# Retention scores as half-height products in one run per head pair, in a kernel of retention, Fourier mixing and an MLP

## The chip, the core and the metric

The kernel runs on one core of a Trainium2 chip. The core has five engines with a queue of instructions each: PE (TensorE, matrix products from SBUF into PSUM; its weight loads are shown as PEld), DVE (VectorE), ACT (ScalarE), POOL (GpSimd) and SP (SyncE, which here only issues DMAs). PSUM has eight banks of 2 KB a partition; a matrix product writes one bank. The metric is the device time in microseconds (us) of one execution, as the median over several runs; lower is better.

## What is computed

Four batches, eight heads, 768 steps, head width 64; a model width of 512 and a hidden width of 2048:

```python
gamma = 1.0 - 2.0 ** (-5.0 - np.arange(H))
for t in range(S):                       # retention, a decayed sum of outer products
    state = gamma * state + einsum('bhd,bhe->bhde', k[:, :, t], v[:, :, t])
    y[:, :, t] = einsum('bhd,bhde->bhe', q[:, :, t], state) / sqrt(D)
x = y, heads side by side                # (4, 768, 512)
u = x + real(fft(fft(x, axis=1), axis=2))
un = (u - mean(u)) / sqrt(var(u) + 1e-6)
out = u + maximum(un @ w_ch1, 0) @ w_ch2
```

The kernel does not run the recurrence step by step. It cuts the 768 steps into six chunks of 128. Within a chunk, y is a masked product of scores (q times k, transposed) with v; what earlier chunks give comes through a state per chunk, built from products of k and v.

## The kernel before

**Order of the work.** Batch one's attention and Fourier part are written out by hand (FIRST). After that the MLP of batch b, two row blocks of 384 rows, is the main stream on PE: 16 hidden products (`h_unit`, 4 matmuls of 384 columns each, evicted with the ReLU to `ht16` by ACT or DVE), then 12 parts of the second layer (`ch_unit`, line 1121, 4 matmuls of 512 columns each, evicted at line 1125 and stored by SP). Between these units, `emit` places the units of batch b+1's attention, its Fourier stages and the normalising. Each stream of units gets a start and an end in units of batches (the tables DM, TS, DA, LD, HT at the top), its units are spread evenly between the two, and all units are emitted in order of the position. Emission is the priority: the framework's scheduler may move an instruction of an engine past one that, by its own reckoning, has to wait. Each engine then works in its fixed order.

**Attention of batches two to four** goes by head pairs (index i from 0 to 3). The steps of `attn_steps` hold: `cast_unit` (POOL: q, k with its decay, v to f16), `kv_unit` (5 products, evicted by one ACT copy and four DVE operations at line 683 that also decay the running state), `y_unit` (22 products of 64 columns into two banks, evicted by two ACT operations at line 716), `t_unit` (q and k transposed) and `a_unit` (scores). In step s stand the cast and the transposes of pair s, the state and scores of pair s-1, and the outputs of pair s-2.

**Scores** (`a_unit`): q transposed is stored as `qTz` in two planes, one for each head of the pair. In each plane the rows of the other head (64 of 128) are zero, so one product of full height, 128 rows by 2 x 128 columns, gives both heads' scores of a chunk at once. There are three parts a pair, spread over time like other units. Each has two such products in a bank and one DVE operation (line 657) that multiplies by the mask and writes the f16 scores `atm`. Batch one has another form (`am_unit`, line 515): products of half height, 64 rows by 128 columns, that use the upper or lower half of the rows for the one or the other head, each head in a bank of its own.

**Transposes** (`t_unit`): in batch two (b < NPE = 2) q and k go through PE (6 transposes each, line 610) and come back by ACT (q in two copies of 64 rows, k in one of 128). In batches three and four two DMA transposes from SP (lines 602 and 604) do it.

**PSUM.** The pool `ps_g` has five banks and serves the scores (`wkA`), `wkK`, `wkY` of batches two to four, the transposes `tq` and `pst`, `ps1` and `pq` of the Fourier stages. `ps_pm` has the other three, for the MLP.

**Second Fourier stage and normalising.** `s2_unit(b, kb)` makes row block kb of u (128 rows): four products, two ACT copies, two DVE sums, two POOL adds of x (lines 1027 and 1029). It then calls `norm_unit`: DVE statistics (lines 1040, 1041) and on ACT the f16 row `un` (line 1042). The buffers of `un` (tag `un16`) are two, in pool `up`. `unT_unit` transposes `un`, by PE for the earlier blocks (line 1065) and by a DMA from SP from block 3 of batch two on (line 1061).

**Loads.** `load_unit` issues the loads of q, k, v of a pair from SP. Those of batch two wait for the seventh weight DMA and a product of batch one; those of later batches wait for `a_of[b - 1, 1]`, the last score product of pair 1 of the batch before.

Of the kernel before, what the change touches and what calls it, by code (L numbers as in the profile page):

```python
# [12 lines left out]
ALU = mybir.AluOpType  # L13
f32 = mybir.dt.float32
f16 = mybir.dt.float16
# [3 lines left out]
P = 128  # L19
B, H, S, D = 4, 8, 768, 64  # L20
DM = 512
DFF = 2048
NCH = S // P
# [6 lines left out]
PAIR_ORDER = [0, 1, 3, 2]  # L30
# [15 lines left out]
"""  # L46
ON_ACT = {'q': (0, 1, 0), 'kv': (1, 1, 1), 'g': (0, 1, 1), 'gr': (0, 0, 0)}
FB = 1
DM0, DM1 = (0.121, 0.179, 0.253, 0.368), (0.004, 0.137, 0.232, 0.341)
TS0 = (0.269, 0.376, 0.393, 0.441, 0.517, 0.575, 0.665, 0.696)  # L50
TS1 = (-0.040, -0.020, 0.048, 0.585)
DA0, DA1 = (0.034, 0.100, 0.173, 0.180, 0.306, 0.315), (0.063, 0.067, 0.063, 0.158, 0.168, 0.189)
LD0, LD1 = (0.160, 0.263), (-0.370, 0.140)
HT0 = (0.683, 0.767, 0.685, 0.583)
NPE = 2
ACT_ROWS = ((2, 5, 6, 7, 8, 9, 10, 14), (0, 3, 6, 7, 9, 10, 11, 12, 14, 15), (2, 4, 5, 6, 7, 8, 10, 14))


@with_exitstack
def kernel(  # L60
# [9 lines left out]
    nc = tc.nc  # L70
# [3 lines left out]
    def pool(name, bufs, **kw):  # L74
        return ctx.enter_context(tc.tile_pool(name=name, bufs=bufs, **kw))
# [9 lines left out]
    fp = pool("fp", 1)  # L85
    gp = pool("gp", 1)
    up = pool("up", 2)
    qnp = pool("qnp", 1)
    hp_ = pool("hp", 1)
    obp = pool("obp", 3)  # L90
    stt = pool("stt", 2)
    ps_g = pool("ps_g", 5, space=PSUM)
# [13 lines left out]
    maskp = const.tile([P, NHP, 2, P], f32, tag="maskp")  # L106
# [71 lines left out]
    in_of, a_of = {}, {}  # L178
# [417 lines left out]
    def t_unit(b, i):  # L596
        def run():
            st = at[b, i] = {}
            kT = st["kT"] = tp.tile([P, NCH, P], f16, tag="kT", name="kT")
            if b >= NPE:  # L600
                qT = st["qT"] = qts[i % 2]
                nc.sync.dma_start_transpose(qT.rearrange("p h c t -> p (h c) t"),
                                            q16_of[b, i].rearrange("p h c d -> p (h c d)"))
                nc.sync.dma_start_transpose(kT, kd_of[b, i].rearrange("p c h d -> p (c h d)"))
                return
            qT = st["qT"] = qts[i % 2] if b else qts[i % 2][:, 0]
            for dst, src in ((qT, q16_of[b, i]), (kT, kd_of[b, i])):
                tq = ps_g.tile([P, NCH, P], f16, tag="g", name="tq", padded_shape=[P, 8, P])
                for c in range(NCH):
                    nc.tensor.transpose(tq[:, c, :], src[:, c].rearrange("p a b -> p (a b)"),  # L610
                                        ident16)
                if dst is qT:
                    for h2 in range(2 if b else 1):
                        rows = slice(D * h2, D * h2 + D) if b else slice(0, P)
                        dst = qT[rows, h2] if b else qT
                        (nc.scalar.copy if h2 == 0 or ON_ACT["q"][min(b, 2)] else nc.vector.tensor_copy)(
                            dst.rearrange("p c t -> p (c t)").rearrange(
                                "p (t c) -> p t c", c=NCH),
                            tq[rows].rearrange("p c t -> p t c"))
                else:  # L620
                    nc.scalar.copy(dst, tq)
        return run
# [23 lines left out]
    def a_unit(b, i, part):  # L646
        def run():
            st = at[b, i]
            if part == 0:
                st["atm"] = ap_.tile([P, NCH, 2, P], f16, tag="atm", name="atm")  # L650
            wk = ps_g.tile([P, 2, 2, P], f32, tag="g", name="wkA")
            for c2 in range(2):
                c = 2 * part + c2
                mm = nc.tensor.matmul(wk[:, c2], st["kT"][:, c, :], st["qT"][:, :, c, :],  # L654
                                      start=True, stop=True)
            a_of[b, i] = mm
            nc.vector.tensor_tensor(  # L657
                out=st["atm"][:, 2 * part:2 * part + 2], in0=wk,
                in1=maskp[:, PAIR_ORDER[i]].unsqueeze(1).to_broadcast([P, 2, 2, P]),
                op=ALU.mult)  # L660
        return run

    def kv_unit(b, i):
# [230 lines left out]
    lb = {}  # L894
# [30 lines left out]
    def n0_unit(half, eng):  # L925
        def run():
            if ("un", 0) not in lb[0]:
                lb[0]["un", 0] = up.tile([P, 2, 257], f16, tag="un16", name="un16").rearrange(
                    "p a b -> p (a b)")[:, 0:DM]
            sl = slice(256 * half, 256 * half + 256)  # L930
            dst, src, mu = lb[0]["un", 0][:, sl], lb[0]["pq", 0][:, sl], fd[0]["mu"][:, 0:1]
            if eng == "a":
                nc.scalar.activation(dst, src, AF.Identity, bias=mu, scale=-1.0)
            else:
                nc.vector.tensor_scalar(out=dst, in0=src, scalar1=-1.0, scalar2=mu, op0=ALU.mult,
                                        op1=ALU.add)
        return run
# [8 lines left out]

    def n_unit(kb, eng):
        def run():
            un = lb[0]["un", kb] = up.tile([P, 2, 257], f16, tag="un16", name="un16").rearrange(
                "p a b -> p (a b)")[:, 0:DM]  # L950
            src, mu = lb[0]["u"][:, kb], lb[0]["st"][:, kb, 0:1]
            if eng == "a":
                lb[0]["una"] = nc.scalar.activation(un, src, AF.Identity, bias=mu, scale=-1.0)
            else:
                lb[0]["una"] = nc.vector.tensor_scalar(out=un, in0=src, scalar1=-1.0, scalar2=mu,
                                                       op0=ALU.mult, op1=ALU.add)
        return run
# [22 lines left out]
    def s2_unit(b, kb):  # L980
        def run():
            if kb == 0:
                lb[b] = dict(u=up.tile([P, NCH, DM], f32, tag="u32", name="u32"),
                             unT=up.tile([P, 4, S], f16, tag="unT", name="unT"),
                             st=stt.tile([P, NCH, 4], f32, tag="stats", name="stats"))
# [11 lines left out]
            if b >= FB:  # L997
                for n, (o, w) in enumerate(((0, 129), (256, 128), (129, 127), (384, 128))):
                    nc.tensor.matmul(pq[:, o:o + w], gt[:, n, j0:j0 + P], t2[:, n, 0:w],  # L999
                                     start=True, stop=True)  # L1000
# [6 lines left out]
                    out=u[:, kb, 0:256].rearrange("p (m t) -> p m t", t=2), in0=lo, scalar=g0,  # L1007
                    in1=qn[:, 0:256].rearrange("p (m t) -> p m t", t=2), op0=ALU.add, op1=op_lo)
                nc.vector.scalar_tensor_tensor(
                    out=u[:, kb, 256:512].rearrange("p (m t) -> p m t", t=2), in0=updn, scalar=g0,  # L1010
                    in1=qn[:, 256:0:-1].rearrange("p (m t) -> p m t", t=2), op0=ALU.add,
                    op1=op_up)
            else:
                for cb in range(2):
                    nc.tensor.matmul(psP, gt[:, cb, j0:j0 + P], cd16[:, cb, 0:257],
                                     start=(cb == 0), stop=(cb == 1))
                for cb in range(2):
                    nc.tensor.matmul(psQ, gt[:, 2 + cb, j0:j0 + P], sd16[:, cb, 1:256],
                                     start=(cb == 0), stop=(cb == 1))
# [8 lines left out]
                                    in1=x[:, kb, 0, 1:257], op=ALU.add)  # L1028
            nc.gpsimd.tensor_tensor(out=u[:, kb, 256:512], in0=u[:, kb, 256:512],  # L1029
                                    in1=x[:, kb, 1, 257:1:-1], op=ALU.add)  # L1030
            norm_unit(b, kb)()
        return run

    def norm_unit(b, kb):
        def run():
            u, stats = lb[b]["u"], lb[b]["st"]
            bst = stt.tile([P, 6], f32, tag=f"bst{kb % 3}", name="bst")
            un = up.tile([P, 2, 257], f16, tag="un16", name="un16").rearrange(
                "p a b -> p (a b)")[:, 0:DM]
            nc.vector.bn_stats(bst, u[:, kb, :])  # L1040
            nc.vector.bn_aggr(stats[:, kb, 0:2], bst)  # L1041
            nc.scalar.activation(un, u[:, kb, :], AF.Identity, bias=stats[:, kb, 0:1], scale=-1.0)  # L1042
            lb[b]["un", kb] = un
        return run
# [12 lines left out]
    def unT_unit(b, kb):  # L1057
        def run():
            un, unT = lb[b].pop(("un", kb)), lb[b]["unT"]
            if b > 1 or b and kb >= 3:  # L1060
                nc.sync.dma_start_transpose(unT[:, :, kb * P:(kb + 1) * P], un)
                return
            pst = ps_g.tile([P, 4, P], f16, tag="g", name="pst", padded_shape=[P, 8, P])
            for cb in range(4):
                nc.tensor.transpose(pst[:, cb, :], un[:, cb * P:(cb + 1) * P], ident16)
            if (kb % 2 == 0) != (b == 0 and kb < 3):
                nc.vector.tensor_copy(unT[:, :, kb * P:(kb + 1) * P], pst)
            else:
                nc.scalar.copy(unT[:, :, kb * P:(kb + 1) * P], pst)
        return run  # L1070
# [162 lines left out]
                    gr=gr_unit, xe=x_edges)[kind](*n)  # L1233

    def mix_units(b, kbs):
        return [s2_unit(b, kb) for kb in kbs], [unT_unit(b, kb) for kb in kbs]

    def emit(streams):
        ev = []
# [19 lines left out]
    for b in range(B):  # L1259
# [17 lines left out]
        if b + 1 < B:  # L1277
            steps = attn_steps(b + 1)
            if b == 0:
# [3 lines left out]
                streams.append(([pad_unit], HT0[2], HT0[3]))  # L1283
                ts = TS0
            else:
                streams.append(([load_unit(b + 1, i) for i in range(4)], b + LD1[0], b + LD1[1]))
                n = [len(u) for u in steps[1:]]
                ts = list(TS1[:2]) + [TS1[2] + TS1[3] * sum(n[:j]) / sum(n) for j in range(6)]
            streams.append((steps[0], b + ts[0], b + ts[1]))
# [38 lines left out]
```

## Time and profile before

| what | value |
|---|---|
| median of 3 runs | 245.68 us (245.26 to 245.90) |
| the profiled execution: its own time | 246.28 us |
| its span, first to last instruction | 244.1 us |
| granted TensorE clock | 1.00 in every stretch |
| score products, line 654 | 72 of 128x256, 57.1 to 174.1 us |
| score evictions, line 657 | 36 of 128x512, 0.680 us each |
| second layer, line 1121 | 89.1 us busy |
| hidden products, line 1078 | 81.9 us busy |
| batch two's attention fed by loads, 52 to 62 us | 258 GB/s, PE busy 8.67 of 10 us |

Times within the execution count from the span's first instruction. A matmul's row overlaps the next one's (its end is modelled, and it is pipelined), so what PE spends on one is read from start to start. In a row of groups, "x6" means six instructions in a row. A row of waits has the engine that waited, the line, who released it, and us in total, how many times, and the longest.

### The profile page before, as it was taken

What the parts mean: (1) busy time and instruction counts of PE and PEld (TensorE: products, weight loads), DVE (VectorE), ACT (ScalarE), POOL (GpSimd) and SP (SyncE); (2) the same over time, 40 slices, a digit from 0 to 9 for tenths busy, and PEclk for the clock granted to TensorE, in tenths of its full rate; (3) what the DMA queues carried; (4) which work ended last, traced back from release to release, by engine and by line L of the source; (5) the groups of instructions that cost most, each with busy time, mean ns of one, the idle gap of its engine ahead of it and who ended that gap; (6) DMA issues with size and microseconds to landing.
All of it is one profiled execution on the core that took longest, in us unless ns stands there. A gap on an engine that the chain in (4) does not pass through costs nothing.

```text
span 244.1 us, 5274 instructions
## 1 busy us (share of the span) xinstructions
PE 231.0 (95%) x2010; PEld 144.6 (59%) x2010; DVE 173.6 (71%) x423; ACT 121.3 (50%) x268; POOL 83.5 (34%) x151
## 2 busy tenths in 40 slices
PE   4499999997999998999999999999999999999995
PEld 1376779755775645665567446665666455445543
DVE  8879987947887788995985748887895556424112
ACT  5989758755785434842247515732257317202500
POOL 7578802456500067690000736660002305000000
PEclk9999999999999999999999999999999999999999
DMA  7997999999999388999999478585100441221012
GB/s 176 232 271 104 199 201 203 221 245 260 268 237 216 69 172 190 182 187 139 262 269 217 92 161 196 118 143 134 72 0 0 46 150 23 43 89 43 1 43 89
DMA packets 99209, 36.39 MB, mean 149 GB/s; under 512 B 89840, under 2 KB 96240, under 8 KB 99184
## 3 DMA queue, kind: packets, MB, share of 16 engines
q1 hardware_dynamic: 94960, 31.86, 63.2%
q0 software_dynamic: 4224, 4.19, 10.8%
q8 instruction: 16, 0.26, 0.5%
q14 instruction: 9, 0.07, 0.1%
HBM read 27.26 MB, written 6.29 MB: 137 GB/s over the span
## 4 chain that ended last, share of the span: by engine, by line
PE 79%; DVE 7%; ACT 4%; DMA 3%; POOL 3%; issue 1%; SPq 1%; POOLq 0%; ACTq 0%; DVEq 0%
PE psc L1121 34%; PE psh L1078 27%; PE wkA L654 3%; DMA v<-in_v_dram 3%; PE ps L837 3%; PE wkY L708 2%; PE pq L999 2%; PE wkY L704 1%; PE wkK L673 1%; PE tq L610 1%; PE ps L817 1%; SPq L209 1%; DVE bst L1040 1%; PE pq L911 1%; DVE atm L529 1%
## 5 line engine op out<-in xcount | busy, mean ns | idle before, releaser
L1121 PE MATMUL psc<-w,ht 128*128 128x512 f16 (+2 forms) x400 | 89.1, 370 | 0.1
L1078 PE MATMUL psh<-unT,w 128*128 128x384 f16 x448 | 81.9, 326 | 0.4 <-ACT ht L1082 0.2
L1121 PEld LDWEIGHTS <-ht 128*128 128x128 f16 x400 | 37.5, 98 | 36.8 <-issue 0.2
L1078 PEld LDWEIGHTS <-w 128*128 128x128 f16 x448 | 42.3, 98 | 24.6 <-issue 1.6
L1082 ACT ACTIVATE ht<-psh 128x384 f16<-128x384 f32 x64 | 30.9, 490 | 40.3 <-PE psh L1078 39.7
L1027 POOL TENSOR_TENSOR u<-u,x 128x256 f32<-128x256 f32 x21 | 13.3, 635 | 106.0 <-DVE u L1006 90.1
L1125 DVE SCALAR_TENSOR_TENSOR ob<-psc,stats,u 128x512 f32<-128x512 f32 (+2 forms) x25 | 18.1, 725 | 25.9 <-PE psc L1121 25.7
L1084 DVE TENSOR_SCALAR ht<-psh 128x384 f16<-128x384 f32 x48 | 26.1, 548 | 8.6 <-PE psh L1078 8.2
L657 DVE TENSOR_TENSOR atm<-wkA,maskp 128x512 f16<-128x512 f32 x36 | 23.9, 683 | 2.5 <-PE wkA L654 2.4
L1042 ACT ACTIVATE un<-u,stats 128x512 f16<-128x512 f32 x21 | 15.1, 721 | 17.9 <-DVE stats L1041 11.5
L683 DVE SCALAR_TENSOR_TENSOR s<-s,gk,wkK 128x128 f16<-128x128 f16 x48 | 16.2, 339 | 6.1 <-ACT s L679 5.5
L1040 DVE BATCH_NORM_STATS2 bst<-u 128x6 f32<-128x512 f32 x21 | 14.6, 694 | 8.3 <-POOL u L1029 8.1
L716 ACT ACTIVATE x<-wkY,gexp 128x384 f16<-128x384 f32 x24 | 12.8, 580 | 9.9 <-PE wkY L708 9.9
L431 POOL TENSOR_SCALAR kd<-k,gexp 128x384 f16<-128x384 f32 x24 | 13.8, 585 | 3.7 <-DMA k<-in_k_dram 2.8
L1029 POOL TENSOR_TENSOR u<-u,x 128x256 f32<-128x256 f32 x21 | 13.3, 635 | 2.4 <-DVE stats L1041 2.4
L654 PE MATMUL wkA<-qTz,kT 128*128 128x256 f16 x72 | 13.3, 273 | 0.1
L1095 PEld LDWEIGHTS <-w 128*128 128x128 f16 x192 | 11.0, 98 | 0.8 <-issue 0.3
L1095 PE MATMUL psh<-unT,w 128*128 128x128 f16 x192 | 11.4, 219 | 0.1
L1001 ACT COPY qn<-pq 128x128 f32<-128x128 f32 x18 | 4.9, 274 | 12.6 <-PE pq L999 11.9
L1006 DVE SCALAR_TENSOR_TENSOR u<-pq,g,qn 128x256 f32<-128x256 f32 x18 | 8.5, 472 | 3.1 <-PE psh L1078 2.5
L436 POOL TENSOR_SCALAR v<-v 128x768 f16<-128x768 f32 x12 | 10.0, 831 | 1.5 <-DMA v<-in_v_dram 1.5
L654 PEld LDWEIGHTS <-kT 128*128 128x128 f16 x72 | 6.9, 98 | 5.6 <-PE psh L1078 0.4
(177 smaller groups left out, 317.4 us busy)
## 6 DMA issues: line engine op xcount, KB each, us to landing
q<-in_q_dram SPq DMA_DIRECT2D x16, 384.0 KB, 6.0
k<-in_k_dram SPq DMA_DIRECT2D x16, 384.0 KB, 6.0
v<-in_v_dram SPq DMA_DIRECT2D x16, 384.0 KB, 6.1
out_dram<-ob SPq DMA_DIRECT2D x23, 256.0 KB, 2.4
w<-in_moe_w_ch_dram POOLq DMA_DIRECT2D x8, 512.0 KB, 11.6
unT<-un SPq DMA_TRANSPOSE x15, 2.4
out_dram<-ob SPq DMA_DIRECT2D x1, 192.0 KB, 1.9
qTz<-q16z SPq DMA_TRANSPOSE x8, 3.8
```

The source lines that it names most:

```text
L431: kc = nc.gpsimd.tensor_scalar(out=kd[:, :, h2, :], in0=k32[:, h2], scalar1=gkd[:, h0 + h2:h0 + h2 + 1], scalar2=1.0, op0=ALU.mult, op1=AL ...
L654: mm = nc.tensor.matmul(wk[:, c2], st["kT"][:, c, :], st["qT"][:, :, c, :], start=True, stop=True)
L657: nc.vector.tensor_tensor(out=st["atm"][:, 2 * part:2 * part + 2], in0=wk, in1=maskp[:, PAIR_ORDER[i]].unsqueeze(1).to_broadcast([P, 2, 2, ...
L683: nc.vector.scalar_tensor_tensor(out=s16[:, c], in0=s16[:, c - 1], scalar=gk2[:, hp:hp + 1], in1=wk[:, c - c0], op0=ALU.mult, op1=ALU.add)
L1040: nc.vector.bn_stats(bst, u[:, kb, :])
L1042: nc.scalar.activation(un, u[:, kb, :], AF.Identity, bias=stats[:, kb, 0:1], scale=-1.0)
L1078: nc.tensor.matmul(psh, w116[:, cb, fb * P:(fb + 1) * P], unT[:, cb, rt * 384:(rt + 1) * 384], start=(cb == 0), stop=(cb == 3))
L1082: nc.scalar.activation(ht16[:, fb, :], psh, AF.Relu, bias=0.0, scale=-1.0)
L1084: nc.vector.tensor_scalar(out=ht16[:, fb, :], in0=psh, scalar1=-1.0, scalar2=0.0, op0=ALU.mult, op1=ALU.max)
L1095: mm = nc.tensor.matmul(psh[:, f], w116[:, cb, fb * P:(fb + 1) * P], unT[:, cb, kb * P:(kb + 1) * P], start=(cb == 0), stop=(cb == 3))
L1121: nc.tensor.matmul(psc[:, c0:c1], ht16[:, fb, rb3 * P:(rb3 + 1) * P], w216[:, fb, c0:c1], start=(fb == 0), stop=(fb == NFB - 1))
L1125: nc.vector.scalar_tensor_tensor(out=ob[:, c0:c1], in0=psc[:, c0:c1], scalar=lb[b]["st"][:, rb, 3:4], in1=lb[b]["u"][:, rb, c0:c1], op0=AL ...
```

## The change

- `a_unit`: part 0 now issues all 12 products of the pair in one run, in the half-height form, into four banks of `ps_g` (three chunks of one head each), and evicts two of them; part 1 evicts the third, part 2 the fourth. Each eviction is 128x384. `a_of`, on which later loads wait, is now the last product of part 0.
- `KD = (3,)`: in batch two, k of pair index 3 is transposed by a DMA from SP; q of that pair stays on PE.
- A pool `unp` of three buffers for `un16`, out of `up`, which had two.
- `s2_unit` no longer calls `norm_unit`. `mix_units` makes turns: turn j issues the sums of the j-th row block, then the normalising of the one before; the last turn issues that of its own block too.
- New numbers in all tables of positions. In order of emission, among others: batch two's pair 1 is transposed one second-layer unit later; batch two's units from kv of pair 2 to the scores of pair 2 stand together without an MLP unit between them; the three DMA transposes of the second half's rows come in reverse order (their stream's end lies before its start); batch one's three last sums stand together.

```diff
-DM0, DM1 = (0.121, 0.179, 0.253, 0.368), (0.004, 0.137, 0.232, 0.341)
-TS0 = (0.269, 0.376, 0.393, 0.441, 0.517, 0.575, 0.665, 0.696)
-TS1 = (-0.040, -0.020, 0.048, 0.585)
-DA0, DA1 = (0.034, 0.100, 0.173, 0.180, 0.306, 0.315), (0.063, 0.067, 0.063, 0.158, 0.168, 0.189)
-LD0, LD1 = (0.160, 0.263), (-0.370, 0.140)
-HT0 = (0.683, 0.767, 0.685, 0.583)
+DM0, DM1 = (0.127, 0.128, 0.261, 0.279), (0.010, 0.137, 0.260, 0.244)
+TS0 = (0.244, 0.368, 0.422, 0.439, 0.519, 0.521, 0.682, 0.695)
+TS1 = (-0.057, 0.016, 0.048, 0.582)
+DA0, DA1 = (0.077, 0.142, 0.177, 0.182, 0.296, 0.312), (0.057, 0.080, 0.086, 0.169, 0.147, 0.204)
+LD0, LD1 = (0.154, 0.258), (-0.365, 0.158)
+HT0 = (0.635, 0.743, 0.599, 0.590)
 NPE = 2
+KD = (3,)
...
+    unp = pool("unp", 3)
...
             for dst, src in ((qT, q16_of[b, i]), (kT, kd_of[b, i])):
+                if dst is kT and i in KD:
+                    nc.sync.dma_start_transpose(kT, src.rearrange("p c h d -> p (c h d)"))
+                    continue
...
             if part == 0:
                 st["atm"] = ap_.tile([P, NCH, 2, P], f16, tag="atm", name="atm")
-            wk = ps_g.tile([P, 2, 2, P], f32, tag="g", name="wkA")
-            for c2 in range(2):
-                c = 2 * part + c2
-                mm = nc.tensor.matmul(wk[:, c2], st["kT"][:, c, :], st["qT"][:, :, c, :],
-                                      start=True, stop=True)
-            a_of[b, i] = mm
-            nc.vector.tensor_tensor(
-                out=st["atm"][:, 2 * part:2 * part + 2], in0=wk,
-                in1=maskp[:, PAIR_ORDER[i]].unsqueeze(1).to_broadcast([P, 2, 2, P]),
-                op=ALU.mult)
+                wk = st["wk"] = [ps_g.tile([P, 3, P], f32, tag="g", name="wkA",
+                                           padded_shape=[P, 4, P]) for _ in range(4)]
+                for c in range(NCH):
+                    for h2 in range(2):
+                        sl = slice(D * h2, D * h2 + D)
+                        mm = nc.tensor.matmul(wk[2 * (c // 3) + h2][:, c % 3],
+                                              st["kT"][sl, c, :], st["qT"][sl, h2, c, :],
+                                              start=True, stop=True)
+                a_of[b, i] = mm
+            for n in ((0, 1), (2,), (3,))[part]:
+                half, h2 = n // 2, n % 2
+                nc.vector.tensor_tensor(
+                    out=st["atm"][:, 3 * half:3 * half + 3, h2], in0=st["wk"][n],
+                    in1=maskp[:, PAIR_ORDER[i], h2].unsqueeze(1).to_broadcast([P, 3, P]),
+                    op=ALU.mult)
...
-            norm_unit(b, kb)()
...
     def mix_units(b, kbs):
-        return [s2_unit(b, kb) for kb in kbs], [unT_unit(b, kb) for kb in kbs]
+        def turn(j):
+            def run():
+                if j < len(kbs):
+                    s2_unit(b, kbs[j])()
+                for n in kbs[max(j - 1, 0):j] + (kbs[-1:] if j == len(kbs) - 1 else []):
+                    norm_unit(b, n)()
+            return run
+        return [turn(j) for j in range(len(kbs))], [unT_unit(b, kb) for kb in kbs]
```

More of the change, by code (lines that the diff above doesn't have):

```diff
@@ L927, in run @@
             if ("un", 0) not in lb[0]:
-                lb[0]["un", 0] = up.tile([P, 2, 257], f16, tag="un16", name="un16").rearrange(
+                lb[0]["un", 0] = unp.tile([P, 2, 257], f16, tag="un16", name="un16").rearrange(
                     "p a b -> p (a b)")[:, 0:DM]
@@ L948, in run @@
         def run():
-            un = lb[0]["un", kb] = up.tile([P, 2, 257], f16, tag="un16", name="un16").rearrange(
+            un = lb[0]["un", kb] = unp.tile([P, 2, 257], f16, tag="un16", name="un16").rearrange(
                 "p a b -> p (a b)")[:, 0:DM]
@@ L1037, in run @@
             bst = stt.tile([P, 6], f32, tag=f"bst{kb % 3}", name="bst")
-            un = up.tile([P, 2, 257], f16, tag="un16", name="un16").rearrange(
+            un = unp.tile([P, 2, 257], f16, tag="un16", name="un16").rearrange(
                 "p a b -> p (a b)")[:, 0:DM]
```

## The prediction

> **What bounds the kernel now.** I read the page's header, its busy shares and the chain of waits first.
>
> ```profile
> span 244.1 us, 5274 instructions
> PE 231.0 (95%) x2010; PEld 144.6 (59%) x2010; DVE 173.6 (71%) x423; ACT 121.3 (50%) x268; POOL 83.5 (34%) x151
> PE 79%; DVE 7%; ACT 4%; DMA 3%; POOL 3%; issue 1%; SPq 1%; POOLq 0%; ACTq 0%; DVEq 0%
> ```
>
> PE holds 79% of the chain that ended last, and the page's forty slices show it at nine tenths or more from the third to the last but one, two excepted. So from about 36 us on, an edit is worth what it takes from PE's issue time, plus what it does to the few waits in which PE stands still. The waits that PE itself or its weight loads had after 46 us come next (waited for, us, times, longest), and with them one DVE row:
>
> ```profile
> PE tq L610 <- POOL kd L431: 1.3, 1, 1.3
> PE pst L1065 <- ACT un L1042: 0.7, 1, 0.7
> PE psh L1078 <- ACT ht L1082: 0.2, 1, 0.2
> PE psh L1078 <- DVE ht L1084: 0.2, 1, 0.2
> PEld L708 <- DVE atm L657: 0.7, 3, 0.3
> DVE bst L1040 <- POOL u L1029: 7.8, 16, 0.9
> ```
>
> Two of them are single holes, one in batch two's attention, one before batch two's second row block. The last row is not PE's, but DVE stands 7.8 us in its queue for POOL, with PSUM evictions behind it. Counted from start to start of PE's matmuls, and with a product charged its columns at the rate of its own undisturbed row (512 columns 0.216 us), I get 6.5 us of PE standing still between 36 us and the end, an estimate. So more than about 6 us cannot come from waits.
>
> **Price of the score products.** The timeline of PE has the old form in batch two (first), and in batch one the half-height form that the change brings (second); columns are start, length, engine, line, operation, tiles, shape.
>
> ```profile
> 57.14 0.38 PE L654 MATMUL wkA<-qTz,kT 128*128 128x256 f16 x2
> 57.36 1.03 PE L1121 MATMUL psc<-w,ht 128*128 128x512 f16 x4
> 58.23 0.60 PE L654 MATMUL wkA<-qTz,kT 128*128 128x256 f16 x4
> 58.66 1.03 PE L1121 MATMUL psc<-w,ht 128*128 128x512 f16 x4
> ```
>
> ```profile
> 19.24 0.59 PE L817 MATMUL ps<-ssp,xab 128*128 128x193 f16 x5
> 19.77 0.51 PE L515 MATMUL wkA<-qTz,kT 64*128 64x128 f16 x12
> 20.21 0.26 PE L817 MATMUL ps<-csp,xab 128*128 128x193 f16 x1
> ```
>
> Old: four products take 58.66 - 58.23 = 0.43 us, so six per head pair 0.65 us. New: the five products of 193 columns ahead of the run start 0.086 us apart (18 of line 837 take 1.54 us in the chain), so they are through at 19.24 + 0.43 = 19.67, and the next full-height product starts at 20.21. The whole run of twelve cost 0.54 us. Six pairs at 0.056 us (128 columns: six transposes start 56.80, the next row 57.14) are 0.34 us, so two half-height products must have run side by side, and about 0.10 us went into each of the change from full to half height and the change back. **Saving: 0.65 - 0.54 = 0.11 us a pair, 12 pairs, 1.4 us.** A broken run is dearer: in batch one a run of six stood 0.24 us between its first two pairs (starts 24.45 and 24.75), and one of twelve some 0.50 us after its seventh (seven products from 15.07 on, the other five from 15.93). With every run broken by 0.24 us the item would turn to +1.5 us. I take three of twelve broken, +0.7 us.
>
> The Trainium skill, "TensorEngine Tiling (Array Packing)", Key Properties, says that a change of the tiling mode drains the array; the two tenths around the run agree with it, and they are why twelve in one run is priced and not three runs of four. By its up to 2x alone, without the drain, the item would be 12 x (0.65 - 0.33) = 3.8 us; the row decides.
>
> **Eviction of the scores.** Before, three operations of 128x512 at line 657, 0.680 us each (2.04 us a pair). After, four of 128x384; the nearest row is line 529, the same width from PSUM with a float mask, 0.547 us (2.19 us). DVE gets 12 x 0.15 = 1.8 us more. What hides it: in 52 to 62 us DVE is busy 5.14 of 10 us, but 8.71 in 62 to 72, 8.29 in 102 to 112 and 9.20 in 150 to 160. Price on PE between 0 and 1.8 us; I take +0.2, since DVE's time comes back partly with the turns below.
>
> **k of pair index 3 of batch two by DMA.** Six transposes of 128 columns leave PE: 6 x 0.057 = 0.34 us, and one ACT copy of 0.80 us. PE no longer waits for that kd cast either (it ended at 66.19 on POOL, and PE reached it at 67.0). SP gets one more transpose: issue 1.2 to 1.95 us, landing 2.7 to 4.6 us by the eight rows of line 604. It stands in SP's queue between batch three's loads and three output stores and waits there for the kd cast. Behind it are the loads of batch three, first needed at about 91 us, and stores that nobody waits for; the buffers of ob are three. Its first reader, the scores of pair 3, starts at 72.2 us, 6 us after the cast. Cover enough: 0 on the path. If it were gone, PE would stand for what is missing of 1.5 + 4.6 us, so up to 1 us. **-0.3 us.**
>
> **Third row buffer.** The hole at 93 us, in the timeline:
>
> ```profile
> 92.30 0.61 PE L1065 MATMUL pst<-ident,un 128*128 128x128 f16 x8
> 92.81 0.72 ACT L1042 ACTIVATE un<-u,stats 128x512 f16<-128x512 f32 x1 [0.47 <-PE pst L1065]
> 93.58 0.40 PE L1065 MATMUL pst<-ident,un 128*128 128x128 f16 x4 [0.68 <-ACT un L1042]
> ```
>
> The third normalised row waits until the first two are transposed, because there are two buffers of un16; its statistics were done at 92.0. With a third buffer it runs at once and ends near 92.75, and two units of new due times lie in between. **-0.7 us** of 0.84. The 1.7 us that ACT waited once for a transpose by DMA goes too, but off the path.
>
> **New turns of the normalising.** The statistics of row block n are now issued after the sums of block n+1, so DVE no longer stands behind POOL's two adds (0.635 us each). What PE lost to this order, by starts: 0.37 us at 203.8 and 0.33 at 208.1 (the two rows with ht above), 0.24, 0.23 and 0.21 between 152 and 156.5: 1.38 us. Bounds 0 and -1.4; I take half, **-0.7**, because the framework already moves such operations past each other. In the third block of each half two rows are normalised in a row, and the first of them is later than before by one turn; the readers (transposes, then 16 hidden products) are four or more products away. The three transposes unT by DMA now go out in reverse, so on SP the last row block's un holds back the two others: about 0.65 x 7 = 4.6 us after its sums, against a chain of 0.95 DVE + 1.3 POOL + 0.9 DVE + 0.72 ACT = 3.9 us. Cover thin, price up to 0.5 us a batch if it fails, taken 0.
>
> **New due times.** Working out the order of emission from both sets of numbers, the first large difference is at the hole of 55 us:
>
> ```profile
> 54.97 0.50 PE L610 MATMUL tq<-ident,q16z 128*128 128x128 f16 x6
> 56.80 0.51 PE L610 MATMUL tq<-ident,kd 128*128 128x128 f16 x6 [1.33 <-POOL kd L431]
> ```
>
> PE stands 1.49 us for the cast of k of pair 1, and that for its load (issued 49.47, median landing 6.0 us, cast started 55.59). The loads are gated by the same weight DMA as before and come no earlier; but pair 1's transposes are emitted one unit of four 512-column products later, which fills 4 x 0.216 = **-0.86 us** of the hole. Against it: batch two's step with kv(2), y(1), t(3) and the scores of pair 2 is now emitted with no large product in between. It needs 2 + 2 + 1 + 4 = 9 banks out of a pool of five. The y banks are freed by two ACT operations of 0.58 us, the kv banks by four DVE operations of 0.34 us. Between nothing (y and transposes, 0.64 + 0.34 us, cover it) and 1.5 us; I take **+0.5**. Batch one's three transposes for row blocks 3 to 5 move ahead of its second product; they cost the same 12 x 0.057 us and their un can be early, since POOL's adds now follow one another: 0. The tables and pads that move by a few units stay in DVE's free time of 72 to 82 us (8.72 of 10 busy): 0.
>
> **Sum.** -1.4 + 0.7 + 0.2 - 0.3 - 0.7 - 0.7 - 0.86 + 0.5 = -2.6 us. The profiled execution took 246.28 us, 244.1 of it span and 2.2 around it, which nothing here changes: 243.7 us. It is 0.6 us over the median of the three runs, 245.68, so against that: **243.1 us**.
>
> **Rivals.** (a) *Banks.* The run takes four of five banks at once, and the last two are evicted one and two units after the first. PE works in order, so a run that waits for a bank holds every product behind it. For it: the two broken runs above, both in batch one. Against it: y is emitted two units ahead of the scores, at about 1 us a unit. All gains without it are 1.4 + 0.3 + 0.7 + 0.7 + 0.86 - 0.2 = 3.8 us; it decides from 3.8 / 12 = 0.31 us a run. At the 0.50 us of the worse row: 245.68 - 3.8 + 6.0 = 247.9 us, slower. The skill's same page, PSUM Bottleneck, warns that faster products leave the eviction as the limit; it would be seen here as this case. (b) *All holes close*: the score saving whole, -1.4 - 0.3 - 0.84 - 1.38 - 1.49 = -5.4, 240.3 us. (c) *The gain moves on*: batch two is fed by loads (258 GB/s in 52 to 62 us), and PE, arriving sooner, waits for the next pair's casts or for DVE: only 0.3 us is left, 245.4 us. Against it: batches three and four show no wait for a load. (d) *The halves do not run side by side*: each run 12 x 0.056 + 0.2 = 0.87 us, so the main sum plus 12 x 0.33 = 4.0: 247.1 us. Against it: the same order and banks as in batch one, where they do.
>
> **How the numbers follow.** Mine 0.50, (a) 0.18, (b) 0.15, (c) 0.13, (d) 0.04. About 0.3% (0.74 us) is what a measurement of this kernel can tell from no change. Faster: mine but for 0.02 that end near the old time, (b), and 0.04 of (c): 0.67. Within: 0.02 and 0.09 of (c): 0.11. Slower: (a) and (d), 0.22. Mine alone spans 241.5 to 244.7. The range goes from the floor of (b), 240.3, to just under (a), 247.2, which leaves out some 0.15.
>
> **What would show it.** Right: score products as pairs of starts some 4 ns apart and runs near 0.54 us; no wait of pst for un; the hole at tq shrunk to about 0.6 us; fewer than 7.8 us of bst waiting for POOL; PE's standing still after 36 us down from 6.5 to about 4 to 5. Wrong: score products with starts broken inside a run, PE waiting for x, s or atm at a score product, or a new PE wait on unT.

## The result, and the profile after

The changed kernel is slower: 246.75 us (median of 5 runs, 246.31 to 247.85) against 245.50 before, a ratio of 1.0052 with a 95% interval of 1.0036 to 1.0068. The profiled execution is the slowest of the five, 247.85 us with a span of 245.7. From its page, the shares by engine and the head of the chain:

```profile
PE 232.8 (95%) x2076; PEld 142.4 (58%) x2076; DVE 175.5 (71%) x435; ACT 120.9 (49%) x267; POOL 83.4 (34%) x151
PE 83%; DMA 5%; DVE 4%; ACT 3%; POOL 1%; SPq 1%; issue 1%; DVEq 0%; ACTq 0%
```

PE was 79% of the chain and is 83%. Three of the forecast's waits are gone, as the waits after 36 us show (first PE's own, then the DVE row):

```profile
PE wkA L661 <- DMA qTz<-q16z: 1.7, 1, 1.7
PE psh L1087 <- ACT ht L1091: 0.3, 1, 0.3
PE pst L1074 <- ACT un L1051: 0.3, 1, 0.3
...
DVE bst L1049 <- POOL u L1039: 2.8, 8, 0.5
```

The hole before k's transposes (1.3 us) is not in the list, pst waits 0.3 us for un and no longer at 93 us, and DVE's statistics (`bst`) wait 2.8 us for POOL where they waited 7.8. In their place stands a wait that no term of the forecast had: a score product, the first of pair 3 of batch three, waits 1.7 us for q transposed by DMA.

```profile
118.28 1.46 PE L1130 MATMUL psc<-w,ht 128*128 128x512 f16 x6
121.44 0.51 PE L661 MATMUL wkA<-qTz,kT 64*128 64x128 f16 x12 [1.70 <-DMA qTz<-q16z]
```

To see where the rest went, I counted PE from start to start of its matmuls, from batch one's first hidden product to the last product of the kernel. A product counts its columns at the rate of its own undisturbed row; "score products" is all time from a score product to the next start and what PE lost right ahead of one, so the changes of height and the waits are in it; "other standing" is what PE lost elsewhere. Times are in us, from the profiled executions.

| kernel | runs come in | score products | other standing | other products |
|---|---|---|---|---|
| before | 33 pieces, full height | 8.25 | 6.24 | 193.37 |
| after | 20 pieces | 11.29 | 4.12 | 193.03 |
| e1 scores only | 19 | 11.53 | 5.24 | 193.37 |
| e2 scores undone | 34, full height | 9.85 | 4.59 | 193.03 |
| e3 later gate | 20 | 9.53 | 4.13 | 193.03 |
| e5 fenced | 12 | 11.59 | 5.19 | 193.03 |
| e8 half where whole | 5 whole, 19 full | 8.64 | 4.01 | 193.03 |
| e9 and loads later | 5 whole, 19 full | 7.67 | 3.96 | 193.03 |

After against before: -2.12 us of standing, -0.34 of other products, and **+3.04 us on the score products**. Ahead of the run that waits for q stand 1.86 us. About 0.10 of this is the change of height that stands ahead of every half-height run (the same holds for such figures below), so 1.77 us is the wait. The two profiled executions differ by two things more: batch one, whose instructions up to there are the same, reached its first hidden product at 33.77 us and not 33.19 (it lies between 33.1 and 34.3 in the profiled executions of all kernels here), and the end is 0.43 us longer (below).

Why the scores cost more stands in PE's timeline of batch two, pair 0 (first) and pair 3 (second):

```profile
57.78 0.34 PE L661 MATMUL wkA<-qTz,kT 64*128 64x128 f16 x6
58.05 0.39 PE L1130 MATMUL psc<-w,ht 128*128 128x512 f16 x1
58.37 0.34 PE L661 MATMUL wkA<-qTz,kT 64*128 64x128 f16 x3
58.64 0.60 PE L1130 MATMUL psc<-w,ht 128*128 128x512 f16 x2
59.18 0.34 PE L661 MATMUL wkA<-qTz,kT 64*128 64x128 f16 x3
59.45 0.39 PE L1130 MATMUL psc<-w,ht 128*128 128x512 f16 x1
```

```profile
72.67 0.51 PE L661 MATMUL wkA<-qTz,kT 64*128 64x128 f16 x12
73.11 0.50 PE L1087 MATMUL psh<-unT,w 128*128 128x384 f16 x2
```

Pair 3's run is whole: 0.44 us, and 0.10 before it. Pair 0's is in three pieces with second-layer products between. Each piece takes 0.27 us, whether it has six products (three pairs side by side) or three (one bank, one half of the rows, no partner), and about 0.10 us ahead: 512 columns starting at 58.05 are through at 58.27, the piece starts at 58.37. That is 3 x 0.37 = 1.1 us, against 0.65 in the old form.

### The profile page after: what moved, and what is told of

Same layout as the page of the kernel before. It is cut to its first block, busy times and chain, and to the rows that moved or that the text cites. A ratio compares the mean times of both kernels' runs of the same rounds, so it can differ in the third digit from the quotient of the medians.

```text
span 245.7 us, 5404 instructions
## 1 busy us (share of the span) xinstructions
PE 232.8 (95%) x2076; PEld 142.4 (58%) x2076; DVE 175.5 (71%) x435; ACT 120.9 (49%) x267; POOL 83.4 (34%) x151
## 4 chain that ended last, share of the span: by engine, by line
PE 83%; DMA 5%; DVE 4%; ACT 3%; POOL 1%; SPq 1%; issue 1%; DVEq 0%; ACTq 0%
PE psc L1130 33%; PE psh L1087 30%; PE wkA L661 3%; DMA v<-in_v_dram 3%; PE ps L847 3%; DMA qTz<-q16z 2%; PE ps L827 2%; PE pq L1009 2%; PE wkY L718 2%; PE wkK L683 1%; PE wkY L714 1%; PE tq L491 1%; PE pq L921 1%; SPq L211 1%; PE tq L615 1%
## 5 line engine op out<-in xcount | busy, mean ns | idle before, releaser
L1087 PEld LDWEIGHTS <-w 128*128 128x128 f16 x448 | 41.4, 98 | 25.9 <-issue 1.2
L667 DVE TENSOR_TENSOR atm<-wkA,maskp 128x384 f16<-128x384 f32 x48 | 24.1, 546 | 1.6 <-PE wkA L661 1.6
L1051 ACT ACTIVATE un<-u,stats 128x512 f16<-128x512 f32 x21 | 14.6, 719 | 11.2 <-DVE stats L1050 7.5
L1104 PEld LDWEIGHTS <-w 128*128 128x128 f16 x192 | 11.1, 98 | 1.2 <-issue 0.7
L661 PE MATMUL wkA<-qTz,kT 64*128 64x128 f16 x144 | 8.7, 218 | 1.8 <-DMA qTz<-q16z 1.7
L661 PEld LDWEIGHTS <-kT 64*128 64x128 f16 x144 | 5.1, 94 | 8.3 <-issue 7.6
L689 ACT CAST s<-wkK 128x128 f16<-128x128 f32 x12 | 3.2, 267 | 11.8 <-issue 8.4
```

Of the source, the lines that this page charges most:

```text
L661: mm = nc.tensor.matmul(wk[2 * (c // 3) + h2][:, c % 3], st["kT"][sl, c, :], st["qT"][sl, h2, c, :], start=True, stop=True)
L667: nc.vector.tensor_tensor(out=st["atm"][:, 3 * half:3 * half + 3, h2], in0=st["wk"][n], in1=maskp[:, PAIR_ORDER[i], h2].unsqueeze(1).to_br ...
L1087: nc.tensor.matmul(psh, w116[:, cb, fb * P:(fb + 1) * P], unT[:, cb, rt * 384:(rt + 1) * 384], start=(cb == 0), stop=(cb == 3))
L1104: mm = nc.tensor.matmul(psh[:, f], w116[:, cb, fb * P:(fb + 1) * P], unT[:, cb, kb * P:(kb + 1) * P], start=(cb == 0), stop=(cb == 3))
```

## The experiments

Each was timed beside the kernel before on the same chip; ratios are to that. Theories: S, broken runs; T, late transposes by DMA; U, batch one's transposes moved ahead of their rows; rivals B (banks) and L (loads).

**e1, the new scores alone in the kernel before.** The edit is the change's `a_unit` and nothing else.

> The kernel before with the new score products alone (runs of twelve half-height products into four banks; old tables, two row buffers, old turns, k by PE). In its order on PE the twelve runs come out in 19 pieces. Theory S (broken runs: a piece costs 0.19 us of change of height, and a piece of three products runs one after the other): products cost 9.2 us against 7.9 of the old form, so 245.5 + 1.3 = 246.8 us. Theory T (the slowdown is the late q transpose of pair 3 of batch three, because the loads of batch four are let go earlier): the gate has moved here too, so up to +1.9 more, or 247.4 alone. The forecast's term (-1.4 saved, +0.7 for broken runs, +0.2 eviction): 245.0 us.

Measured: 248.89 us, 1.0138 (1.0124 to 1.0152). The score part alone loses 3.3 us, two more than its pieces; the rest is PE standing in or ahead of runs. T is not it: no wait for a transpose of q is in the profile. The longest stop, by the timelines of PE and ACT:

```profile
107.05 0.39 PE L656 MATMUL wkA<-qTz,kT 64*128 64x128 f16 x7
108.93 0.32 PE L656 MATMUL wkA<-qTz,kT 64*128 64x128 f16 x5 [1.49 <-ACT x L721]
```

```profile
107.68 0.72 ACT L1047 ACTIVATE un<-u,stats 128x512 f16<-128x512 f32 x1 [1.41 <-DMA unT<-un]
108.31 0.57 ACT L721 ACTIVATE x<-wkY,gexp 128x384 f16<-128x384 f32 x1
```

The run wants the bank of an output y; y's eviction stands on ACT behind a normalised row, and that row waits 1.41 us for one of two row buffers, which a transpose by DMA still reads. The four-bank run thus ties PE to SP's queue. The changed kernel, with its third row buffer, has no such wait in its profile; that the buffer alone cuts the tie was not tested.

**e2, the old scores in the changed kernel.**

> The changed kernel with the old score products (three parts of two full-height products; everything else of the change kept). Theory S: 246.75 - 1.6 = 245.1 us. Theory T: the load gate is the old one again, so the 1.86 us of the wait for q transposed go as well: 243.3 us with both, 244.9 with T alone. The forecast's term: the score part was a gain, so 247.2 us.

Measured: 245.94 us, 1.0014 (1.0004 to 1.0024). Most of the loss goes with the scores. But T's part of the expectation was wrong: with the old gate PE still waits 0.95 us for q transposed at 118 us. Of the 1.44 us between the two rows of the table, 0.8 is that shorter wait and 0.6 the products: in this order of work full-height scores stand for other things too (8.90 us without the wait, against 8.25 before).

**e3, a later gate for the loads.**

```diff
-                a_of[b, i] = mm
-                nc.vector.tensor_tensor(
+                a_of[b, i] = nc.vector.tensor_tensor(
```

> The changed kernel, with the loads of the next batch gated by the last score eviction of pair 1 in place of the last product of its run; SP's order then has the q transpose of pair 3 of batch three ahead of one load more, as before the change. Theory T: the wait of PE for q transposed, 1.86 us in the profile, shrinks below 0.7 us, 245.3 to 246.0 us. Theory S: nothing of its cost is touched, 246.75 us within 0.4.

Measured: 246.19 us, 1.0019 (1.0005 to 1.0032), and in the profile nothing is left of the 1.86 us. SP's issues, after (first) and here:

```profile
112.83 1.23 SPq L606 DMA_TRANSPOSE kT<-kd  x1
114.10 0.57 SPq L191 DMA_DIRECT2D q<-in_q_dram  x1
114.73 0.72 SPq L191 DMA_DIRECT2D k<-in_k_dram  x1
115.54 3.77 SPq L604 DMA_TRANSPOSE qTz<-q16z  x1
```

```profile
112.60 1.23 SPq L606 DMA_TRANSPOSE kT<-kd  x1
113.92 0.53 SPq L191 DMA_DIRECT2D q<-in_q_dram  x1
114.55 2.76 SPq L604 DMA_TRANSPOSE qTz<-q16z  x1
```

With two loads ahead the transpose landed 5.8 us after its issue, at 121.3, when PE had been ready since 119.6. With one ahead it was issued 1.0 us earlier and landed after 5.2; without loads ahead (pair 3 of batch four) it takes 3.7. T is shown. It is worth 0.6 us by the medians and 0.8 by the ratios, less than the wait in the profiled execution, which was the slowest of its five.

**e4, three row buffers and turns alone.**

> The kernel before with three row buffers and the new turns of the normalising alone. Forecast's terms: -0.7 (third buffer, the hole at 93 us) and -0.7 (turns), so 244.1 us. Rival: the framework's order had hidden the turns already and the third row is late for another reason, 245.3 us or more.

Measured: 245.41 us, 0.9994 (0.9986 to 1.0003): no difference. The hole at 93 us is gone, and the one at 55 us is 0.74 us (in this execution PE reached it 0.5 us later and was let go 0.3 us earlier). But products of y wait for score evictions, 0.81 us at 155 and 0.36 at 103; the kernel before stood 0.23 and 0.21 us near 156 and not at 103. It looks as if the turns moved DVE's time from one reader to another; buffer and turns were not timed apart.

**e5, whole runs by force.** Each PE instruction emitted after a run is ordered behind its last product:

```diff
+            for x in tc.nc.cur_bb.bb.instructions[n0:]:
+                if run_end and str(x.engine) == run_end[0]:
+                    tc.add_manual_dep(x, run_end[1],
+                                      mybir.DependencyInfo(mybir.DependencyClass.NoSync,
+                                                           mybir.DependencyReason.DATA),
+                                      reason="behind the run")
```

> The changed kernel, in which every PE instruction emitted after a run of twelve stays behind its last product. In its order on PE all twelve runs are whole (20 pieces before). Theory S (broken runs): the products cost 12 x 0.54 = 6.4 us in place of 9.4, PE does not wait for banks, 243.8 us, or 244.9 with the wait for q transposed still there in full. Rival B (banks: the run was broken because a bank was not free, so a whole run waits as long as its pieces cost): PE waits 0.3 us or more inside most of the eight runs that were broken, 246.4 us or more.

Measured: 248.61 us, 1.0127 (1.0107 to 1.0147). Rival B holds. (Six runs were broken in the changed kernel, not eight as written there.) The runs are whole in order, but PE stands inside four of these six: 0.39 and 0.30 us in pair 0 of batch two, 0.64 in pair 1, 0.31 in pair 2, and in pair 0 of batch four

```profile
151.35 0.34 PE L661 MATMUL wkA<-qTz,kT 64*128 64x128 f16 x6
151.99 0.34 PE L661 MATMUL wkA<-qTz,kT 64*128 64x128 f16 x3 [0.30 <-ACT ht L1092]
153.12 0.32 PE L661 MATMUL wkA<-qTz,kT 64*128 64x128 f16 x3 [0.80 <-DVE u L1020]
```

(The first of the two waits names ACT's `ht`, which frees a bank of the MLP's pool. A DVE operation on the state ended at the same 151.94 us and frees one of `ps_g`, so it may be that one.) So the pieces were not a whim of the order: four of five banks are not free when most of these pairs are due. Standing costs more than breaking: without the wait for q the score products take 10.8 us here and 9.5 in pieces. The Trainium skill, "TensorEngine Tiling (Array Packing)", PSUM Bottleneck, warns that tiling speeds up the products and not the eviction; these waits for evictions agree.

**e6, batch one's old due times.** `DM0 = (0.121, 0.179, 0.253, 0.368)` in the changed kernel, where batch one's transposes and the product behind them wait for their rows, as the profile after has it:

```profile
45.98 0.39 PE L1074 MATMUL pst<-ident,un 128*128 128x128 f16 x4
46.64 0.34 PE L1074 MATMUL pst<-ident,un 128*128 128x128 f16 x3 [0.27 <-ACT un L1051]
47.12 1.05 PE L1104 MATMUL psh<-unT,w 128*128 128x128 f16 x16
```

> The changed kernel with the old due times of batch one's last three row blocks alone (DM0). Theory U (batch one: the transposes moved ahead wait for their rows, 0.43 + 0.31 + 0.13 us at 45 to 47 us): 245.9 us. Rival L (loads: batch two's hole at 55 us was a wait for loads that come no earlier, so what PE loses before it is not lost at the end): 246.75 us within 0.4, and the hole at batch two's first k transposes is there again.

Measured: 246.64 us, 1.0038 (1.0021 to 1.0054). Other standing falls from 4.12 to 3.25 us as U says, but the time hardly moves (0.1 us by the medians, 0.3 by the ratios, and the intervals overlap). L was wrong about the place: the hole at 55 us did not come back. PE, earlier, waits for two transposes by DMA, 0.68 us at 111 (a new wait, for k) and 1.05 at 119 (for q); e10 tests whether the gain is lost there.

**e7, half height only where the run is whole.** Five pairs as in the change, the other seven in the old form (`if (b, i) not in ((1, 3), (2, 2), (2, 3), (3, 2), (3, 3))`, batches counted from 0).

> The changed kernel with half-height products only for five of the twelve pairs (pair 3 of batch two, pairs 2 and 3 of batches three and four), which come out whole in the order on PE; the other seven in the old form. Theory S: 245.94 of the kernel with the old scores less 5 x 0.12 us = 245.4 us. Rival B: these runs too are paid in waits, 245.9 us or more.

Measured: 245.67 us, 0.9994 (0.9981 to 1.0008), between the two; PE waits 1.11 us for q transposed again.

**e8, e7 with batch one's old due times.**

> The kernel of e7 with the old due times of batch one's last three row blocks. Theories S and U together: 245.4 - 0.87 = 244.5 us, below both kernels. Rivals B and L: 245.4 to 245.9 us.

Measured: 244.64 us, 0.9950 (0.9933 to 0.9968). S and U together, as expected. The wait for q is still there, 1.17 us.

**e9, e8 with batch four's loads behind that transpose.** The edit moves these loads and nothing else:

```diff
-                    tc.add_manual_dep(dma.ins, a_of[b - 1, 1].ins.name,
+                    tc.add_manual_dep(dma.ins, a_of[b - 1, 2 if b == 3 else 1].ins.name,
```

> The kernel of e8, with the loads of batch four gated by the scores of pair 2 of batch three in place of pair 1, so that SP issues the q transpose of pair 3 ahead of the first of these loads. Theory T: it lands within about 4 us of its issue in place of 5.3, the wait of 1.17 us before the scores of pair 3 falls below 0.3, 243.6 us. Rival: batch four's loads are late in turn, or the transposes before it set the landing, 244.6 us within 0.4.

Measured: 243.94 us, 0.9939 (0.9927 to 0.9951), the best of all and 1.5 us under the kernel before. Against e8 it is 0.7 us by the medians and 0.3 by the ratios, whose intervals overlap; the wait itself is gone from the profile. SP's issues and PE's waits after 36 us:

```profile
110.34 2.52 SPq L606 DMA_TRANSPOSE kT<-kd  x1
112.95 1.30 SPq L604 DMA_TRANSPOSE qTz<-q16z  x1
114.34 0.98 SPq L191 DMA_DIRECT2D q<-in_q_dram  x1
```

```profile
PE wkY L737 <- DVE atm L664: 0.5, 2, 0.2
PE psh L1106 <- ACT ht L1110: 0.3, 1, 0.3
PE ps L910 <- DVE xg L901: 0.2, 1, 0.2
```

The transpose lands 4.5 us after its issue, not 3.7, but in time: no score product waits for it.

**e10, e3 and e6 together** (all pairs at half height).

> The changed kernel (half-height products for all pairs) with both the later gate of e3 and batch one's old due times of e6. If T and U add: 246.75 - 0.6 - 0.9 = 245.2 us. If what batch one gives is lost again at the transposes by DMA, as e6's profile has it (0.7 and 1.05 us of new waits at 111 and 119 us): 246.0 us or more.

Measured: 245.26 us, 0.9982 (0.9970 to 0.9994). They add: of the two waits at which e6 lost its gain, 0.07 us is left, at 119. The later gate accounts for that one; why the one at 111 is gone too is not shown. T and U together undo the whole slowdown. In the changed kernel the broken runs alone do not make the time longer than before; they eat what the rest of the change gives.

**e11, e8 with k of pair 3 on PE.** `KD = ()`.

> The kernel of e8 with k of pair 3 of batch two transposed on PE again. The forecast's term: +0.3 us, 244.95 us. Rival: SP and the DMA queue are what is short in batch two, so the DMA transpose cost as much as it gave, 244.6 us or less.

Measured: 244.62 us, 0.9964 (0.9952 to 0.9976), against 0.9950 (0.9933 to 0.9968) of e8. The intervals overlap and the medians are all but equal: not settled. The profiles show why little is left of the gain. PE's 0.34 us are there, and in e11 PE stands 0.50 us for k at 65 us. But from the first product of the last second-layer stage to the end e8 takes 13.90 us and e11 13.46, and the wait for q transposed, in e8 (first), is not in e11:

```profile
119.00 0.51 PE L680 MATMUL wkA<-qTz,kT 64*128 64x128 f16 x12 [1.01 <-DMA qTz<-q16z]
```

```profile
118.74 0.51 PE L680 MATMUL wkA<-qTz,kT 64*128 64x128 f16 x12
```

There q's transpose landed at 117.3 us, and in e8 at 118.9. The profiled execution of e8 is 0.7 us longer than that of e11, for all that its PE had less to do.

**e12, e8 with the old scores for all pairs.**

> The kernel of e8 with the old score products for all pairs. Theory S: five whole runs fewer at 0.12 us, 244.64 + 0.6 = 245.2 us. Rival: the half height gave nothing even where the run is whole, 244.6 us or less.

Measured: 244.98 us, 0.9977 (0.9966 to 0.9989), against 0.9950 of e8. Five whole runs give 0.3 us by the medians and 0.7 by the ratios, whose intervals just touch; 5 x 0.12 = 0.6 was expected. e7 against e2, the same step, gives 0.3 and 0.5. In the profiles the scores take 7.6 us in e8 and 8.4 here, the wait for q left out. Where the run is whole, the half height pays.

## Why the prediction was wrong, by its steps

- **Price of the score products: this step failed.** The price of a whole run was right: 0.44 + 0.10 = 0.54 us. The count was wrong. I took three of twelve runs broken, at 0.24 us each, and the profile has six broken into 14 pieces. And a break does not cost a wait of 0.24 us; it costs another change of height and back, 0.19 us, and it leaves products without a partner, which then take 0.056 us each and not 0.056 us for two. The term was -1.4 + 0.7 = -0.7 and came out as 11.29 - 1.77 - 8.25 = **+1.3 us** (+0.6 against e2, whose old scores stand in the same order of work). I had worked out that one of the new steps needs nine banks of five and priced it as a wait of 0.5 us of its own. It was the same shortage in six pairs: in e5, by the rows of the waits, runs of theirs wait for evictions of a state, of the scores before or of a Fourier sum.
- **Rival (a), banks**, named the right mechanism, with a chance of 0.18. In e5, where nothing hides it, PE stands 3.1 us inside the runs. With the products that lose their partner by it, the twelve runs take 4.2 us more than whole ones, 0.35 a run and over the 0.31 from which it was to decide; in the changed kernel the order pays for it with pieces instead.
- **k by DMA:** -0.34 us of products, as reckoned. What I had not looked for is the rest of SP's work, above all the end. From the end of the last DVE operation to the end of the span it takes 2.52 us before and 2.94 after. In the program the DMAs of SP count on eight semaphores in turn, and the end waits for each in order. With one DMA more, the last store is on the first of them and not on the last, so the seven other waits, 0.06 us each in the trace, come after its landing and not before it. e8 against e11, which differ in this DMA alone, shows the same 0.44 us. From the start of the last product to the end it takes 3.11 to 3.14 us in all four kernels without this DMA (before, e1, e4, e11) and 3.55 to 3.57 in all ten with it.
- **Loads and SP's queue:** I looked at what stands behind the added transpose in SP's queue, and not at what the earlier last score product (`a_of`) lets go. It lets the loads of batch four go ahead of a transpose that PE waits for: 1.8 us of waiting in the profile, 0.6 to 0.8 in the median (e3). This was the forecast's blind spot. The gate is not the whole of it: with the old gate, e2, e7, e8 and e12 still stand 0.95 to 1.17 us there, and before, e1, e4 and e11, which have no DMA for k, not at all (e1 even with the new gate, but PE came later there). I had written "cover enough: 0 on the path" for that DMA; e8 against e11 speaks against it, with one profile each.
- **Third row buffer** (-0.7): right, the hole of 0.84 us at 93 us is gone. **New due times** (-0.86 of 1.49 us at 55 us): the whole hole went, in e2 too, where batch one's first hidden product came as early as before (33.1 us). **Turns** (-0.7): bst waits 2.8 us and not 7.8, but e4 finds buffer and turns together at no difference; by its profile DVE's time comes back as waits for the scores `atm`. **Batch one moved ahead** (taken as 0): 0.43 + 0.31 + 0.13 us lost, worth 0.9 us in e10 against e3 and 1.0 in e8 against e7. All of "other standing" came out at -2.1 us; without the scores the forecast had -0.7 - 0.7 - 0.86 + 0.5 + 0.2 = -1.6.
- **The miss as a whole**, between the profiled executions: the forecast had -2.6 us and the span grew by 1.6. Of these 4.2 us the score products are 2.0, the wait for q 1.8, the later end 0.4 and batch one's unchanged start, which varies by itself, 0.6; other standing came out 0.6 better.
- **Eviction** (+0.2): the size was right, 0.546 us each by the profile; its own price on PE can't be told apart from the banks.
- Rival (c), that the gain moves on to a later wait, is what e6 and e10 show, and it seems e11, at transposes by DMA in place of loads. Rival (d) fell: halves run side by side wherever both are in one piece.

What stays open: how the gain of the whole runs is shared between products and evictions; whether k by DMA pays once q's transpose is in time, as in e9; and why an unchanged start takes 33.1 us in some executions and up to 34.3 in others.

## What to carry to other kernels

A product form that is faster only in a whole run, as here, needs all its PSUM banks at once, so before pricing it, go through the order and count, for each run, who held these banks last and when they are evicted; a scheduler that breaks the run takes the gain back with each piece. When the end of a step serves as the gate of other transfers, an earlier end lets those transfers go earlier, and what matters is what they now stand ahead of. A gain ahead of a late transfer shows only once that transfer is mended, so try such edits in pairs (e6 alone gave 0.1 to 0.3 us, with e3 it gave 0.9).

## What the runs showed of the hardware that was not expected

- Three half-height products of one half take as long as six in pairs: 0.27 us from the first start to the next full-height one, in either case.
- The DMA transpose of q of pair 3 landed 3.7 to 3.8 us after its issue in batch four, with no load just ahead of it on SP's queue, in all kernels. In batch three it took 4.5 us in e9, 5.0 to 5.7 in the nine kernels with one load of 384 KB just ahead, and 5.5 to 6.2 in the four with two.
- One DMA more on SP, long before, made the end 0.42 to 0.44 us longer (before and after, e11 and e8).
